# Small token group of a fused attention and expert kernel: the order of Vector and Scalar work within a slot

## The chip, the cores and the metric

The kernel runs on one core of one Trainium2 chip, in one launch. The metric is the device time of that core in microseconds (us). Five engines matter: TensorE (PE in the profile, with its weight loads PEld), VectorE (DVE), ScalarE (ACT), GpSimd (POOL, idle here) and SyncE (SP), which issues the DMAs. Each engine takes its instructions in the order in which the program gives them, and they meet through semaphores.

## What is computed

Attention through 32 packed tokens, then a dense layer with silu, then eight experts. A Sinkhorn iteration over all tokens gives the weight P of each token and expert.

```python
p_packed = sm_attn(p, k, v); out = sm_attn(q, p_packed, p_packed)     # 2304 x 512
h = x @ w_in;  x = (h * sigmoid(h)) @ w_out
P = exp(x @ w_gate - max)
for _ in range(8):
    P /= P.sum(1, keepdims=True) + 1e-9
    P /= P.sum(0, keepdims=True) + 1e-9
    P *= N / E
for e in range(8):
    out += P[:, e:e+1] * (max(x @ w1[e], 0) @ w2[e])
```

All of it is float32. The kernel gets the accuracy from pairs of float32r matmul operands: a tile is split into `hi` (a cast by ACT) and `lo` (raw minus `hi`, by DVE).

## The kernel before

The stages follow each other: attention with the start of the dense layer, the dense layer, the **small group** (from 374 to 560 us of the span), and then two groups of 1024 tokens with a Strassen-like scheme of seven products to the end. Only the small group is changed. In the dense layer a preparation `pre0` makes the first pieces for it.

The small group is 256 tokens (two tiles of 128). It runs 16 steps s = 0 to 15, one for each expert e = s // 2 and half fh = s % 2 of the hidden width. Each step has four slots, 0 to 3, and a piece number j = slot // 2. The order of all instructions of PE, DVE and ACT is the order of the Python code here (a manual schedule).

- PE, slots 0 and 2: `up0(s, j)`, 32 matmuls (L1011 with 512 columns, L1014 with 256) into a PSUM tile `u`. PE, slots 1 and 3: `down0(s-1, j)`, 12 matmuls (L1046) into `d`: the two hidden pieces `h` of the step before, in the order hi, hi, lo for each quarter of the width.
- `sum0(s, j)`, in slots 0 and 2: ACT copies half of `u` into `us` (L1020), DVE adds the other half (L1021).
- `relu0(s, j)`, in slots 1 and 3: ACT writes the relu of `us` as the hi part of `h` (L1030), DVE writes its lo part (L1031). The second piece, h(s, 1), is made in slot 3 of step s, and the first matmul that needs its lo part is the ninth of `down0(s, 0)` in slot 1 of step s + 1.
- Weight pieces: `w1_split` and `w2_split` give one piece a slot: an ACT cast (`w1h`, `w2h`, L144), a DVE subtraction (`w1l`, `w2l`, L145), and the DMA that loads the next raw piece. The piece made in slot 0 is w1(s+1, 1), in slots 1 and 2 w2(s, 0) and w2(s, 1), in slot 3 w1(s+2, 0).
- `sinkhorn` is a generator `sk` that moves on by one piece in every odd slot from step 1 on. In steps 2 to 6 a piece is: PE sums the columns of P with a matmul (`cs`, L1259), DVE takes the reciprocal `rc` (L1261, L1262), scales P (L1263), sums rows (L1252 to L1254), scales again (L1255) and sums columns (`csum`, L1256), which the next `cs` matmul reads half a step later. The row sum of iteration 0 has to wait for ACT's exp of P (L1248).
- `acc`: after `down0` with an odd s - 1, ACT copies `d` (experts 0 to 2, L1053) or DVE adds P times `d` (from expert 3 on, L1061; L1058 and L1060 collect the older ones in step 8).
- `x_forms`, a generator `xg`, from step 8 on in slots 1 to 3: DVE differences `xr` (L956 to L965), an ACT cast to `xf` (L977) and a DVE subtraction for its lo part (L978), for the next token group.

In the order before, an odd slot of a step holds: `down0` with its `acc`, the Sinkhorn piece, the weight piece, `relu0`, the piece of `xg`. An even slot holds `up0`, the weight piece, `sum0`, the piece of `xg`.

Of the kernel before, what the change touches and what calls it, by code (L numbers as in the profile page):

```python
# [9 lines left out]
F32 = mybir.dt.float32  # L10
# [4 lines left out]
ALU = mybir.AluOpType  # L15
# [89 lines left out]
def fused_kernel(  # L105
# [15 lines left out]
    pe, dve, act = nc.tensor, nc.vector, nc.scalar  # L121

    def pool(name, bufs, **kw):
        st = ExitStack()
        return st.enter_context(tc.tile_pool(name=name, bufs=bufs, **kw)), st
# [14 lines left out]
    def unit(shape, dt, name):  # L140
        return wp.tile(shape, dt, tag="w", name=name)

    def split(hi, lo, raw, eng=dve):
        act.copy(out=hi, in_=raw)  # L144
        eng.tensor_tensor(out=lo, in0=raw, in1=hi.bitcast(F32), op=ALU.subtract)  # L145
# [607 lines left out]
    G0 = 2 * NE  # L753
# [10 lines left out]
    raw1, raw2, wf, xf = {}, {}, {}, {}  # L764
# [8 lines left out]
    def load_w1(s, kh):  # L773
        _, e, fh = steps[s]
        t = st["r1"].tile([128, 2, FH], F32, tag="r1", name=f"r1_{s}{kh}")
        nc.sync.dma_start(t, w1[e, 256 * kh:256 * kh + 256, FH * fh:FH * fh + FH]
                          .rearrange("(c p) f -> p c f", p=128))
        raw1[s, kh] = t
# [64 lines left out]
    w1t, w2t = {}, {}  # L843

    def halves(name, s, j, raw):
        h = unit([128, 2, 512], F32R, f"{name}h{s}{j}")
        l = unit([128, 2, 512], F32R, f"{name}l{s}{j}")
        split(h, l, raw)
        return h, l

    def w1_split(s):
        w1t[s] = []
        for j in range(2):
            w1t[s].append(halves("w1", s, j, raw1[s, j]))
            if s + 1 < G0:
                load_w1(s + 1, j)
            yield
# [31 lines left out]
    def w2_split(s):  # L889
        w2t[s] = []  # L890
        for j in range(2):
            w2t[s].append(halves("w2", s, j, raw2[s, j]))
            if s + 1 < G0:
                load_w2(s + 1, j)
            yield
# [93 lines left out]
    xs, h0, done0 = [], {}, set()  # L989

    w1s = {s: w1_split(s) for s in range(G0)}
    w2s = {s: w2_split(s) for s in range(G0)}

    def pre0():

        xs.append(st["xx"].tile([128, 4, 2, 256], F32R, tag="xx", name="xs"))
        for k in range(4):
            for n, (sb, c, _) in enumerate(T0):
                o = slice(128 * n, 128 * n + 128)
                split(xs[0][:, k, 0, o], xs[0][:, k, 1, o], x2[sb][k][:, c:c + 128])  # L1000
            yield
        for g, n in ((w1s, 0), (w1s, 0), (w2s, 0), (w2s, 0), (w1s, 1)):
            next(g[n])
            yield

    def up0(s, j):
        ps = st["u0"].tile([128, 2, 512], F32, tag="u0", name=f"u0{s}{j}")
        for i in range(2):
            f = slice(128 * (2 * j + i), 128 * (2 * j + i) + 128)
            for k in range(4):  # L1010
                pe.matmul(ps[:, i], w1t[s][k // 2][0][:, k % 2, f], xs[0][:, k].rearrange("p l n -> p (l n)"),  # L1011
                          start=(k == 0), stop=(k == 3), skip_group_check=True)
            for k in range(4):
                pe.matmul(ps[:, i, 0:256], w1t[s][k // 2][1][:, k % 2, f], xs[0][:, k, 0],  # L1014
                          start=False, stop=(k == 3), skip_group_check=True)
        h0[s, j] = ps

    def sum0(s, j):
        u0, ps = st["S"].tile([128, 2, 256], F32, tag="S", name=f"us{s}{j}"), h0[s, j]
        act.copy(out=u0, in_=ps[:, :, 256:])  # L1020
        dve.tensor_tensor(u0, ps[:, :, 0:256], u0, op=ALU.add)  # L1021
        h0[s, j] = u0

    def relu0(s, j):
        if (s, j) in done0:
            return
        done0.add((s, j))
        u0 = h0[s, j]
        t = st["gh"].tile([128, 2, 2, 256], F32R, tag="gh", name=f"h0{s}{j}")
        act.activation(t[:, 0], u0, AF.Relu)  # L1030
        dve.scalar_tensor_tensor(t[:, 1], u0, 0.0, t[:, 0].bitcast(F32), op0=ALU.max, op1=ALU.subtract)  # L1031
        h0[s, j] = t
# [3 lines left out]
    def down0(s, tt):  # L1036
        _, e, fh = steps[s]
        if fh == 0:
            ps0[tt] = p3.tile([128, 512], F32, tag="y", name=f"d0{s}{tt}")
        ps = ps0[tt]  # L1040
        n = 0
        for f in range(4):
            wh, wl = w2t[s][f // 2]
            h = h0[s, f // 2]
            for l, w in ((0, wh), (0, wl), (1, wh)):
                pe.matmul(ps, h[:, l, f % 2, 128 * tt:128 * tt + 128], w[:, f % 2],  # L1046
                          start=(fh == 0 and n == 0), stop=(fh == 1 and n == 11))
                n += 1
        if fh == 0:
            return  # L1050
        if e < LATE:
            acc[e, tt] = st["acc"].tile([128, DM], F32, tag="acc", name=f"acc{e}{tt}")
            act.copy(out=acc[e, tt], in_=ps)  # L1053
            return
        pr = prob["P"][:, T0[tt][2], :]
        dst = acc[0, tt]
        if e == LATE:
            dve.tensor_scalar_mul(dst, dst, pr[:, 0:1])  # L1058
            for i in range(1, LATE):
                dve.scalar_tensor_tensor(dst, acc[i, tt], pr[:, i:i + 1], dst, op0=ALU.mult, op1=ALU.add)  # L1060
        dve.scalar_tensor_tensor(dst, ps, pr[:, e:e + 1], dst, op0=ALU.mult, op1=ALU.add)  # L1061
        if e == NE - 1:
            nc.sync.dma_start(out[128 * tt:128 * tt + 128, :], dst)
# [270 lines left out]
    with tc.manual_schedule(engines={mybir.EngineType.PE, mybir.EngineType.DVE, mybir.EngineType.Activation}):  # L1334
        for i, (c, b) in enumerate(seq):
# [14 lines left out]
            for half in range(2):  # L1350
# [25 lines left out]
                while len(tiles) > keep:  # L1376
                    n = tiles.pop(0)
# [46 lines left out]
    with tc.manual_schedule(engines={mybir.EngineType.PE, mybir.EngineType.DVE, mybir.EngineType.Activation}):  # L1424
        sk = sinkhorn()
        next(sk)
        for g in (1, 2):
            for k in range(4):
                tc.keep_in_program_order(nc.sync.dma_start(
                    x2d[k, :, TOK[g]:TOK[g] + 2 * NB],  # L1430
                    x2[2 - g][k][:, TOK[g] % SB:TOK[g] % SB + 2 * NB]))
        for s_ in (a2a_st, x2a_st, x2b_st, gt_st, hp_st, pt_st, pg_st):
            s_.close()
        for name, n in (("xf", 7), ("cp", 5), ("xr", 2), ("pb", 2)):
            open_(name, n, side="left", keep=True)
        open_("acc", 2 * LATE)
        st["u0"], u0_st = pool("pu", 2, space=PSUM, side="left", reuse_waits="tile")

        def chain(*gens):
            for g in gens:  # L1440
                yield from g

        xg = x_forms(1, x_keep, 3)
        for s in range(G0 + 1):
            for slot in range(4):
                if slot % 2 == 0:
                    if s < G0:
                        up0(s, slot // 2)
                elif s > 0:
                    if s == 2 * LATE + 2 and slot == 1:  # L1450
                        for _ in sk:
                            pass
                    down0(s - 1, slot // 2)
                if s == G0:
                    continue
                if s >= 1 and slot % 2:
                    next(sk, None)
                g, n = ((w1s, s + 1), (w2s, s), (w2s, s), (w1s, s + 2))[slot]
                if n < G0:
                    next(g[n], None)  # L1460
                if slot % 2 == 0:
                    sum0(s, slot // 2)
                if slot % 2 or s == G0 - 1:
                    relu0(s, slot // 2)
                if s >= 8 and slot:
                    next(xg, None)
            if s == G0 - 2:
                for _ in xg:
                    pass
            if s == G0 - 2:  # L1470
                for p in ORD[:2]:
                    w1_block(G0, p, "S")
            if s == G0 - 3:
                load_pb(1, 0)
            if s == G0 - 1:
                for p in ORD[:AHEAD]:
                    w1_get(G0, p)
        for name in ("acc", "r2", "gh", "xx", "po"):
            closers[name].close()
        u0_st.close()  # L1480
        st["m"], s_ = pool("pm", 2, space=PSUM, side="left", reuse_waits="tile"); ctx.enter_context(s_)
        for name, n in (("hb", 6), ("hi", 3), ("lo", 3), ("rb", 2)):
            open_(name, n, keep=True)
        forms = chain(*(w2_forms(s) for s in range(G0, 2 * G0)))
        xg2 = [x_forms(2, x_store)]
        moe_step(G0)
# [56 lines left out]
```

## Time and profile before

| | |
|---|---|
| time, median of 3 runs | 1785.2 us (1785.18 to 1785.34) |
| the profiled execution's own time | 1785.38 us |
| its span (first to last instruction) | 1783.6 us |
| PE busy | 1767.4 us, 99% of the span |
| PE weight loads | 1495.9 us, 84% |
| DVE busy | 1455.1 us, 82% |
| ACT busy | 1083.8 us, 61% |
| granted TensorE clock | 0.999 |

Matmuls are pipelined, and their ends are modelled: a matmul of 512 columns shows some 390 ns, while the next one starts 230 ns later. So PE can be late without showing idle time; the distance from one start to the next tells more. On DVE, too, an instruction that waits for nothing starts up to 0.09 us before the recorded end of the one before it.

### The profile page before, as it was taken

Reading aid. Unit: us, or ns where it says so; the run is one execution under the profiler, and the core shown is the slowest. Engines: PE = TensorE matmul, PEld = TensorE weight load, DVE = VectorE, ACT = ScalarE, POOL = GpSimd, SP = SyncE. Lnnn points to the kernel's source line nnn. Section 1 sums busy time; section 2 is a strip of 40 time slices with the busy share of each in tenths; the row PEclk is TensorE's granted clock in tenths of the full one; section 3 lists DMA queues with packets and bytes.
Section 4 is the critical chain, followed back from the end, with each engine's and each line's share of the span. In section 5 each row is a group of like instructions: output and inputs, shape, how many; then the busy total and the mean of one; then the engine's idle time right before and its main releaser. Section 6 shows DMA issues by size and latency. Waiting matters only on the chain.

```text
span 1783.6 us, 24891 instructions
## 1 busy us (share of the span) xinstructions
PE 1767.4 (99%) x9324; PEld 1495.9 (84%) x9324; DVE 1455.1 (82%) x1950; ACT 1083.8 (61%) x1726; POOL 1.0 (0%) x8
## 2 busy tenths in 40 slices
PE   8999999999999999999999999999999999999998
PEld 5899999987888888888888888888888888888887
DVE  7968796769886988999889999887777777777778
ACT  6766675655654666665666666656555555555555
POOL 0000000000000000000000000000000000000000
PEclk9999999999999999999999999999999999999999
DMA  9326676975764655465554455964455444545442
GB/s 359 132 95 214 248 264 248 334 251 167 227 199 166 226 182 187 160 197 190 195 168 171 172 182 197 323 224 166 155 176 158 161 154 147 168 157 170 149 130 94
DMA packets 141496, 341.72 MB, mean 192 GB/s; under 512 B 11952, under 2 KB 49472, under 8 KB 140480
## 3 DMA queue, kind: packets, MB, share of 16 engines
q1 hardware_dynamic: 141376, 340.14, 56.1%
q8 instruction: 73, 1.20, 0.3%
q14 instruction: 47, 0.39, 0.1%
HBM read 256.66 MB, written 83.44 MB: 191 GB/s over the span
## 4 chain that ended last, share of the span: by engine, by line
PE 91%; DVE 5%; ACT 1%; DMA 1%; issue 1%; SPq 0%; DVEq 0%; ACTq 0%
PE d L1134 34%; PE X L1182 20%; PE Z L1182 10%; PE g2w L689 8%; PE g L600 5%; PE Y L1182 5%; PE d L1046 3%; PE g L654 3%; PE u L1011 2%; PE u L1014 1%; DVE w2l L145 1%; PE u L193 1%; DMA kq<-in_kT_dram 1%; DVE w1l L145 0%; DMA rawin<-in_moe_w_in_dram 0%
## 5 line engine op out<-in xcount | busy, mean ns | idle before, releaser
L145 DVE TENSOR_TENSOR lo<-hb,hi 128x1024 fp32r<-128x1024 f32 x224 | 273.6, 1221 | 33.2 <-ACT hi L144 32.3
L1134 PE MATMUL d<-hi,w2f 128*128 128x512 f32 x896 | 294.2, 389 | 0.0
L1182 PE MATMUL X<-xf,w1l 128*128 128x512 f32 x1152 | 276.9, 389 | 0.0
L144 ACT CAST hi<-hb 128x1024 fp32r<-128x1024 f32 x224 | 235.3, 1052 | 65.3 <-PE d L1134 60.0
L1182 PEld LDWEIGHTS X<-xf,w1l 128*128 128x128 f32 x1152 | 216.2, 188 | 44.9
L1142 ACT COPY M<-d 128x512 f32<-128x512 f32 x234 | 137.3, 588 | 143.6 <-PE d L1134 140.6
L1146 DVE TENSOR_TENSOR M<-d,M 128x512 f32<-128x512 f32 x204 | 140.2, 688 | 101.3 <-PE d L1134 101.3
L1134 PEld LDWEIGHTS d<-hi,w2f 128*128 128x128 f32 x896 | 168.1, 188 | 34.8
L1134 PE MATMUL d<-lo,w2f 128*128 128x512 f32 x448 | 174.3, 389 | 0.0
L1134 PE MATMUL d<-hi,w2l 128*128 128x512 f32 x512 | 167.7, 389 | 0.0
L689 PE MATMUL g2w<-ring,woh 128*128 128x384 f32 x576 | 147.5, 337 | 0.0
L1130 ACT COPY d<-M 128x512 f32<-128x512 f32 x216 | 127.1, 589 | 20.4 <-DVE M L1146 19.0
L1134 PE MATMUL d<-hi,w2g 128*128 128x512 f32 x384 | 125.7, 389 | 0.0
L1134 PEld LDWEIGHTS d<-hi,w2l 128*128 128x128 f32 x512 | 96.1, 188 | 20.4 <-ACT d L1130 0.4
L689 PEld LDWEIGHTS g2w<-ring,woh 128*128 128x128 f32 x576 | 102.9, 188 | 8.6 <-issue 7.5
L1189 ACT COPY cp<-X 128x512 f32<-128x512 f32 x128 | 74.3, 581 | 47.1 <-PE X L1182 46.9
L1134 PE MATMUL d<-lo,w2l 128*128 128x512 f32 x256 | 99.6, 389 | 0.0
L1134 PEld LDWEIGHTS d<-lo,w2f 128*128 128x128 f32 x448 | 84.2, 188 | 17.4
L1182 PE MATMUL Y<-xf,w1f 128*128 128x512 f32 x384 | 97.3, 389 | 0.0
L689 PE MATMUL g2w<-ring,wol 128*128 128x384 f32 x288 | 96.3, 334 | 0.0
L144 ACT CAST w1f<-rb 128x512 fp32r<-128x512 f32 x96 | 59.8, 624 | 55.9 <-PE d L1134 41.3
L1182 PE MATMUL X<-xf,w1f 128*128 128x512 f32 x384 | 92.2, 389 | 0.0
(222 smaller groups left out, 3428.0 us busy)
## 6 DMA issues: line engine op xcount, KB each, us to landing
r<-in_moe_w_dram SPq DMA_DIRECT2D x128, 512.0 KB, 4.2
w1l<-w1d SPq DMA_DIRECT2D x128, 512.0 KB, 3.8
w1d<-po SPq DMA_DIRECT2D x64, 512.0 KB, 4.3
w2d<-w2f SPq DMA_DIRECT2D x64, 512.0 KB, 4.1
w2l<-w2d SPq DMA_DIRECT2D x64, 512.0 KB, 3.5
rb<-in_moe_w_dram SPq DMA_DIRECT2D x96, 256.0 KB, 2.6
sb<-in_moe_w_dram SPq DMA_DIRECT2D x48, 256.0 KB, 2.7
pb<-pd SPq DMA_DIRECT2D x16, 512.0 KB, 5.1
```

What stands on the lines that cost most here:

```text
L144: act.copy(out=hi, in_=raw)
L145: eng.tensor_tensor(out=lo, in0=raw, in1=hi.bitcast(F32), op=ALU.subtract)
L600: pe.matmul(ps, lhs[:, fs], rhs, start=(n == 0), stop=(n == 5))
L654: pe.matmul(ps[:, :HS], lhs, rhs, start=(n == 0), stop=(n == 3 * nf - 1))
L689: pe.matmul(ps[:, :TW], lhs[:, f % 2, ds], ring[f // 2][:, 2 * (f % 2) + rhs, q], start=(n == 0 and not on), stop=(n == 11), skip_group_ch ...
L1046: pe.matmul(ps, h[:, l, f % 2, 128 * tt:128 * tt + 128], w[:, f % 2], start=(fh == 0 and n == 0), stop=(fh == 1 and n == 11))
L1130: act.copy(out=ps, in_=m)
L1134: pe.matmul(ps, w[:, l, c, 128 * d:128 * d + 128], r[:, c], start=(n == 0 and not seed), stop=(n == 5), skip_group_check=seed)
L1142: act.copy(out=m, in_=ps)
L1146: dve.tensor_tensor(m, ps, m, op=ALU.add)
L1182: pe.matmul(ps, w[:, l, c, 128 * i:128 * i + 128], x[:, r, c], start=(n == 0 and p in (1, 7)), stop=(n == 5), skip_group_check=p in (2, 6, ...
L1189: act.copy(out=t, in_=ps)
```

## The change

The split of a weight piece becomes two generator steps: ACT's cast, then the DVE subtraction with the next load. A slot now holds, in program order: `up0` (even slots), the cast of the weight piece, `relu0` (odd slots), the subtraction of the weight piece, the piece of `xg`, `sum0` (even slots), and last, in odd slots, `down0` with its `acc` and the Sinkhorn piece. `pre0` calls each generator twice, so that its instructions stay as they were.

```diff
     def halves(name, s, j, raw):
-        split(h, l, raw)
+        act.copy(out=h, in_=raw)
+        yield
+        dve.tensor_tensor(out=l, in0=raw, in1=h.bitcast(F32), op=ALU.subtract)
         return h, l
...
-            w1t[s].append(halves("w1", s, j, raw1[s, j]))
+            w1t[s].append((yield from halves("w1", s, j, raw1[s, j])))
...
         for g, n in ((w1s, 0), (w1s, 0), (w2s, 0), (w2s, 0), (w1s, 1)):
+            next(g[n])
             next(g[n])
             yield
...
             for slot in range(4):
-                if slot % 2 == 0:
-                    if s < G0:
-                        up0(s, slot // 2)
-                elif s > 0:
+                odd, j = slot % 2, slot // 2
+                g, n = ((w1s, s + 1), (w2s, s), (w2s, s), (w1s, s + 2))[slot]
+                g = g[n] if n < G0 else iter(())
+                if s < G0:
+                    if not odd:
+                        up0(s, j)
+                    next(g, None)
+                    if odd:
+                        relu0(s, j)
+                    next(g, None)
+                    if s >= 8 and slot:
+                        next(xg, None)
+                    if not odd:
+                        sum0(s, j)
+                        if s == G0 - 1:
+                            relu0(s, j)
+                if odd and s > 0:
                     if s == 2 * LATE + 2 and slot == 1:
                         for _ in sk:
                             pass
-                    down0(s - 1, slot // 2)
-                if s == G0:
-                    continue
-                if s >= 1 and slot % 2:
-                    next(sk, None)
-                g, n = ((w1s, s + 1), (w2s, s), (w2s, s), (w1s, s + 2))[slot]
-                if n < G0:
-                    next(g[n], None)
-                if slot % 2 == 0:
-                    sum0(s, slot // 2)
-                if slot % 2 or s == G0 - 1:
-                    relu0(s, slot // 2)
-                if s >= 8 and slot:
-                    next(xg, None)
+                    down0(s - 1, j)
+                    if s < G0:
+                        next(sk, None)
```

The order of PE's own matmuls stays as it was; only numbers of buffers differ. What moves is DVE and ACT. DVE between two `csum` of the Sinkhorn steps (slot 3 of step 2 to slot 1 of step 3), before:

```order
L1256 TENSOR_REDUCE csum<-P 128x8
L145 TENSOR_TENSOR w1l_4769<-r_40_4651,w1h_4768 128x1024
L1031 SCALAR_TENSOR_TENSOR h_4774<-us_4740,h_4774 128x512
L145 TENSOR_TENSOR w1l_4795<-r_41_4677,w1h_4794 128x1024
L1021 TENSOR_TENSOR us_4800<-u_4777,us_4800 128x512
L1261 TENSOR_SCALAR rc<-cs_4816 128x8
```

The same place on DVE in the changed program:

```order
L1259 TENSOR_REDUCE csum<-P 128x8
L850 TENSOR_TENSOR w1l_4795<-r_41_4677,w1h_4794 128x1024
L1024 TENSOR_TENSOR us_4800<-u_4777,us_4800 128x512
L1034 SCALAR_TENSOR_TENSOR h_4806<-us_4800,h_4806 128x512
L850 TENSOR_TENSOR w2l_4804<-r_30_4689,w2h_4803 128x1024
L1264 TENSOR_SCALAR rc<-cs_4825 128x8
```

The kinds are the same five; `h` now stands directly behind the `us` that it is made from, where before the Sinkhorn piece and a weight piece stood between them.

ACT from the `us` copy of step 4, slot 0, before:

```order
L1020 COPY us_4918<-u_4895 128x512
L1053 COPY acc_4933<-d_4803 128x512
L144 CAST w2h_4946<-r_40_4831 128x1024
L1030 ACTIVATE h_4952<-us_4918 128x512
L144 CAST w2h_4972<-r_41_4857 128x1024
```

ACT there in the changed program:

```order
L1023 COPY us_4918<-u_4895 128x512
L848 CAST w2h_4921<-r_40_4810 128x1024
L1033 ACTIVATE h_4924<-us_4918 128x512
L1056 COPY acc_4942<-d_4812 128x512
L848 CAST w2h_4972<-r_41_4857 128x1024
```

ACT's copy of `d`, which needs the end of `down0`, has moved behind the cast and the relu.

DVE in step 10, from the `us` of its first piece to that of its second, before:

```order
L1021 TENSOR_TENSOR us_5574<-u_5551,us_5574 128x512
L1061 SCALAR_TENSOR_TENSOR acc_4694<-d_5473,P,acc_4694 128x512
L145 TENSOR_TENSOR w2l_5591<-r_100_5490,w2h_5590 128x1024
L1031 SCALAR_TENSOR_TENSOR h_5596<-us_5574,h_5596 128x512
L956 TENSOR_TENSOR xr_5392<-xr_5392 128x512
L978 TENSOR_TENSOR xf_5548<-xr_5393,xf_5548 128x512
L145 TENSOR_TENSOR w2l_5621<-r_101_5518,w2h_5620 128x1024
L1021 TENSOR_TENSOR us_5626<-u_5603,us_5626 128x512
```

And in the changed program, with the `h` behind the second piece:

```order
L1024 TENSOR_TENSOR us_5574<-u_5551,us_5574 128x512
L1034 SCALAR_TENSOR_TENSOR h_5580<-us_5574,h_5580 128x512
L850 TENSOR_TENSOR w2l_5578<-r_100_5480,w2h_5577 128x1024
L958 TENSOR_TENSOR xr_5376<-xr_5376 128x512
L980 TENSOR_TENSOR xf_5535<-xr_5377,xf_5535 128x512
L1064 SCALAR_TENSOR_TENSOR acc_4703<-d_5484,P,acc_4703 128x512
L850 TENSOR_TENSOR w2l_5621<-r_101_5518,w2h_5620 128x1024
L961 TENSOR_TENSOR xr_5376<-xr_5377,xr_5376 128x512
L980 TENSOR_TENSOR xf_5587<-xr_5376,xf_5587 128x512
L1024 TENSOR_TENSOR us_5630<-u_5603,us_5630 128x512
L1034 SCALAR_TENSOR_TENSOR h_5636<-us_5630,h_5636 128x512
```

`acc` has moved behind the x difference, the second difference and its `xf` have moved ahead of the second `us`, and again each `h` follows its `us`.

## Rows read from the trace of the kernel before

**Rows 1.** Page, engines: busy us (share of the span), instructions.
```profile
PE 1767.4 (99%) x9324; PEld 1495.9 (84%) x9324; DVE 1455.1 (82%) x1950; ACT 1083.8 (61%) x1726; POOL 1.0 (0%) x8
```

**Rows 2.** Waits of all engines, 365 to 560 us: total, times, longest.
```profile
PE d L1046 <- DVE h L1031: 2.5, 4, 1.0
```

**Rows 3.** Timeline of PE: start us, us, instruction, idle before it.
```profile
407.82 0.39 PE L1046 MATMUL d<-w2l,h 128*128 128x512 f32 x1
409.18 0.73 PE L1046 MATMUL d<-w2h,h 128*128 128x512 f32 x2 [0.97 <-DVE h L1031]
...
446.33 0.48 PE L1011 MATMUL u<-xs,w1h 128*128 128x512 f32 x1
...
463.29 0.61 PE L1011 MATMUL u<-xs,w1h 128*128 128x512 f32 x2
...
474.38 0.62 PE L1011 MATMUL u<-xs,w1h 128*128 128x512 f32 x2
...
514.10 0.74 PE L1046 MATMUL d<-w2h,h 128*128 128x512 f32 x2 [0.83 <-DVE h L1031]
...
548.74 0.62 PE L1011 MATMUL u<-xs,w1h 128*128 128x512 f32 x2
```

**Rows 4.** Chain that ended last, 400 to 450 us: start us, us, what.
```profile
401.30 1.22 DVE w2l L145
...
443.29 1.22 DVE w1l L145
...
445.16 1.20 PE d L1046 x4
```

**Rows 5.** Stretches: us, busy of PE, PEld, DVE, ACT, POOL; clock, DMA, GB/s.
```profile
404.70:446.70 42.00, 40.57 (x207) 33.30 (x206) 40.31 (x85) 22.25 (x31) 0.00 (x0) 1.00 0.57 178
466.90:547.00 80.10, 78.75 (x396) 65.91 (x395) 68.94 (x89) 47.94 (x69) 0.00 (x0) 1.00 0.63 193
```

**Rows 6.** Timeline of DVE, one round of the Sinkhorn steps.
```profile
410.77 0.16 DVE L1261 TENSOR_SCALAR rc<-cs 128x8 f32<-128x8 f32 x1
...
413.29 1.22 DVE L145 TENSOR_TENSOR w2l<-r,w2h 128x1024 fp32r<-128x1024 f32 x1
414.42 0.69 DVE L1031 SCALAR_TENSOR_TENSOR h<-us,h 128x512 fp32r<-128x512 f32 x1
415.02 1.22 DVE L145 TENSOR_TENSOR w2l<-r,w2h 128x1024 fp32r<-128x1024 f32 x1
416.16 0.69 DVE L1021 TENSOR_TENSOR us<-u,us 128x512 f32<-128x512 f32 x1
416.76 0.16 DVE L1261 TENSOR_SCALAR rc<-cs 128x8 f32<-128x8 f32 x1
```

**Rows 7.** Timeline of DVE in steps 2, 8, 14 and 15.
```profile
399.65 0.42 DVE L1252 TENSOR_REDUCE rsum<-P 128x18 f32<-128x144 f32 x1 [1.88 <-ACT P L1248]
...
466.94 0.69 DVE L1021 TENSOR_TENSOR us<-u,us 128x512 f32<-128x512 f32 x1 [1.64 <-ACT us L1020]
...
546.95 0.69 DVE L1031 SCALAR_TENSOR_TENSOR h<-us,h 128x512 fp32r<-128x512 f32 x1
...
548.17 0.68 DVE L1021 TENSOR_TENSOR us<-u,us 128x512 f32<-128x512 f32 x1
549.55 0.69 DVE L1031 SCALAR_TENSOR_TENSOR h<-us,h 128x512 fp32r<-128x512 f32 x1 [0.70 <-ACT h L1030]
```

**Rows 8.** Timeline of ACT in step 15.
```profile
548.88 0.63 ACT L1030 ACTIVATE h<-us 128x512 fp32r<-128x512 f32 x1 [1.49 <-DVE us L1021]
```

**Rows 9.** Waits of DVE, 466.9 to 547 us: total, times, longest.
```profile
DVE w1l L145 <- ACT w1h L144: 3.7, 5, 1.0
DVE w2l L145 <- ACT w2h L144: 3.5, 4, 1.0
DVE us L1021 <- ACT us L1020: 2.8, 3, 1.6
DVE acc L1061 <- PE d L1046: 2.4, 2, 1.4
```

More of the change, by code (lines that the diff above doesn't have):

```diff
@@ L891, in w2_split @@
         for j in range(2):
-            w2t[s].append(halves("w2", s, j, raw2[s, j]))
+            w2t[s].append((yield from halves("w2", s, j, raw2[s, j])))
             if s + 1 < G0:
```

## The prediction

> **What bounds the kernel now.** I read the page first. PE is busy 99% of the span [rows 1], so only two things can change the time: a wait that PE has in the small group, or one that it gets. The waits of all engines from 365 to 560 us come next. PE waits there four times, 2.5 us in all, each time for DVE's lo part of `h` [rows 2]. The timeline of PE shows what such a wait costs: between the starts at 407.82 and 409.18 lie 1.36 us, where the next matmul normally starts after 0.23, so 1.13 us are lost and 0.97 recorded [rows 3]. An undisturbed step takes 474.38 - 463.29 = 11.09 us [rows 3].
>
> The chain of waits says more than PE's idle time. From 401.30 to PE's restart at 445.16 it runs over DVE [rows 4]. In the stretch 404.7 to 446.7 DVE is busy 40.31 of 42.00 us [rows 5], and its timeline there shows a round of half a step that waits for nothing: from `rc` to `rc` 416.76 - 410.77 = 5.99 us [rows 6]. PE's restarts at 409.18 and 445.16 [rows 3, 4] lie 35.98 us apart, which is six such rounds (35.94). So in steps 3 to 6 **DVE sets the pace**, and PE's small waits are only where this shows. In steps 8 to 15 DVE is busy 68.94 of 80.10 us [rows 5] and has waits of its own [rows 9]; PE waits there too, as at 514.10 [rows 3].
>
> **The change part by part.** PE's own order stays; its matmuls cost the same.
>
> *What it removes.* The lo part of h(s, 1) no longer stands behind a Sinkhorn piece and a weight piece. From `us` to `h` the round of before takes 0.60 (us) + 2.52 (the piece, 410.77 to 413.29) + 1.13 (weight) = 4.25 us [rows 6]. The four waits of PE [rows 2] go as long as DVE is no later than now. If every delay of PE went: in steps 8 to 15 PE takes 548.74 - 463.29 = 85.45 us [rows 3] for seven and a half steps of 11.09, 83.18, so 2.3 is to be had there; in the Sinkhorn steps 1.1 for the first wait plus at most 3 x (11.98 - 11.09) = 2.7, part of which is PE's own `cs` matmuls. That makes 3.4 to 6.1; I take the middle, 4.7.
>
> *What it adds.* `h` on DVE needs ACT's relu, which needs DVE's `us`. Before, DVE worked on something else while ACT did that relu. Now `h` is the next DVE instruction, and DVE has nothing to do until it comes. The trace has this order at one place, step 15: `us` starts at 548.17, the relu at 548.88 (0.63 us), `h` at 549.55, with 0.70 us of recorded idle time [rows 7, 8]. Start to start that is 1.38 us, where a DVE that waits for nothing needs 0.60 (414.42 to 415.02, the same size of work) [rows 6]. **Each `h` therefore costs DVE 0.78 us more**, twice a step. Queued behind it on DVE are the weight piece, the Sinkhorn piece or the x pieces, and for these PE waits through `csum` and through the next `h`. Where DVE has slack this costs nothing; the rows above say that in steps 2 to 6 it has none.
>
> *Term A, the Sinkhorn steps.* The exp chain is left as it is: the row sum at 399.65 still waits for ACT's exp [rows 7], and the `csum` of iteration 0 ends as before, when DVE goes on at 401.30 [rows 4]. From there to the `csum` of iteration 7 before were seven rounds, 443.29 - 401.30 = 41.99 us [rows 4]. A round now is 5.99 + 0.78 = 6.77 us; seven are 47.4, so this `csum` ends at 448.7. PE's next `cs` matmul needs it, and behind `cs` stands `up0(6, 1)`, which began at 446.33 [rows 3]. PE reached `cs` on its own by then, so it waits: with 0.2 us for `cs` itself the start is 448.9, and **A = +2.6 us**. It is less than 7 x 0.78 = 5.5 because PE now meets DVE at `csum`, at the end of a round, and `h` comes early in it. Bounds: if the 0.78 were hidden, PE would be free and A would be -2.4 (the Sinkhorn half of the 4.7); if PE and DVE met no later than before, +5.5.
>
> *Term B, steps 8 to 15.* At `us` of step 8 (466.94) DVE had waited 1.64 us for PE's result [rows 7], so there it is again at PE's pace and B starts from zero. The end point is `h` of (14, 1) at 546.95 [rows 7], for which PE's `down0` waits before `up0(15, 1)` at 548.74 [rows 3]. These 80.0 us of DVE hold 12.4 - 1.64 = 10.8 us of recorded waits, 13 of them [rows 9]; each also loses the 0.09 by which an instruction otherwise starts before the recorded end of the last one (414.42 against 413.29 + 1.22 [rows 6]), so 12.0. In the new order:
> - 14 `h` at 0.78 each: +10.9.
> - At (10, 1), (13, 1) and (14, 1) an x difference now stands ahead of ACT's `us` copy, so DVE's `us` waits for `xf` and the copy. The like wait where a cast stands in the copy's place is 1.0 [rows 9], and the copy handles half the elements; so about 0.6 each, an estimate: +1.8.
> - One `acc` (the one of step 14, slot 3) moves behind the end point: -0.7.
> - Of the 12.0 old waits, those for PE's results and most of those for casts go, since DVE is later and ACT does its cast during the wait for the relu. Those stay where an x difference still stands ahead of a cast: I count five, two at 1.1 and three at 0.4 with `acc` between, 3.4 us. So -8.6.
>
> The sum is **B = +3.4 us**. With nothing saved but the recorded waits for PE it could be near +9; if DVE never came late, PE would lose its old waits and B = -2.3. I take +3.4: DVE's 69 us of work in 80 [rows 5] with 14 forced waits of 0.78 leave no slack.
>
> **Edits at nothing.** ACT's copy of `d` moves behind cast and relu; in the Sinkhorn steps DVE lags half a step behind ACT, which hides it, and without that cover DVE would wait for the late cast, up to 1.0 us a time, as it now does elsewhere [rows 9]. Loads of raw pieces are issued 0.6 us later in odd slots; the pieces are needed a step, 11 us, later. The `yield` in `pre0` moves no instruction.
>
> **Sum.** 1785.38 (the profiled execution's own time) + 2.6 + 3.4 = 1791.4 us; it stands 0.2 above the median of the runs, so 1791.2. Nothing behind step 15 gives it back, as PE is the bound there.
>
> A rule that would have it otherwise stands in the Trainium skill, Perfetto Trace Analysis, Optimization Strategy: find the gaps of the engine that one optimizes, see what blocks them, and make these dependencies start sooner. Read on PE, the engine with the highest occupancy here, it speaks for this change and gives the -4.7 of the first rival. The rows disagree as to which engine that is: the chain is DVE's in steps 3 to 6, and the page itself allows that the most contended engine changes over time. Against the change speaks what TensorE: Matmul & The Clock Gate, Architectural detail, says: the queues of ACT and DVE are strictly first in, first out; the 0.70 us of idle DVE with other work in line [rows 7] agrees.
>
> **The rivals.**
> 1. *The waits for `h` go and nothing comes in their place:* 1785.2 - 4.7 = 1780.5. For it: all four waits are for `h` [rows 2], and `h` is ready 4.25 - 1.38 = 2.9 us earlier after its `us`. Against it: DVE without slack. It decides where the 0.78 a half step is covered, that is if PE's half step with `cs` were over 6.77 us.
> 2. *Only the Sinkhorn steps lose:* in steps 8 to 15 the earlier `h` and the extra waits cancel, B between -2.3 and +1. Time 1785.5 to 1788.8, middle 1787.2. For it: DVE is idle 11 us of 80 there [rows 5, 9]. Against it: those waits are forced by ACT and partly remain.
> 3. *More is lost:* old waits stay in full, or ACT's copy of `d` holds up casts; B about +9, time 1797.
> 4. *Nothing to measure because the order does not bind:* excluded by rounds without a wait [rows 6], but for small cancellation, held in 2.
>
> **How the numbers follow.** Forecast (1788.8 to 1794.5, around 1791.2) 0.6; rival 2 0.2; rival 1 0.12; rival 3 0.08. A measurement of this kernel tells some 0.2%, 3.6 us, from no change. Slower by more: the forecast, rival 3 and a little of 2, less the forecast's lower edge, 0.66; within: 0.22; faster: 0.12. The range 1786.0 to 1794.5 leaves out rival 1, rival 3 and the edge of 2.
>
> **What would show it.** In the changed kernel's trace: DVE idle about 0.70 us before each `h`, ended by ACT (right: the added wait). PE's waits at `cs` for `csum`, about 1 us per half step from step 3 to 6, and none for `h` there; rounds of 6.77 us; `up0(6, 1)` at 448.9 (term A). In steps 8 to 15 PE waits for `h` in steps 12 and 15, 2 to 3 us each (term B); `up0(15, 1)` at about 554.7. The prediction is wrong if rounds stay near 6 us, or if PE never waits at `cs`.

## The result and the profile after

The changed kernel takes 1794.4 us (median of 6 runs, 1793.36 to 1795.64); the kernel before, run beside it, 1785.36 us. The ratio is 1.0051, 95% interval 1.0038 to 1.0064: **slower by 9.0 us**. The forecast was slower, +6.0 us.

The engines of the page after, in busy us (share of the span) and instructions, beside [rows 1]:

```profile
PE 1769.2 (99%) x9324; PEld 1495.9 (83%) x9324; DVE 1456.0 (81%) x1950; ACT 1083.5 (60%) x1726; POOL 1.0 (0%) x8
```

The instruction counts are those of before, so no engine has more work. The waits of all engines from 365 to 560 us (total, times, longest) say where the time is, and stand against the single group of PE before [rows 2]:

```profile
DVE h L1034 <- ACT h L1033: 22.7, 31, 1.3
...
PE d L1049 <- ACT h L1033: 5.7, 3, 2.7
...
PE cs L1262 <- DVE csum L1259: 3.5, 5, 0.7
```

DVE now waits 22.7 us in 31 places for the relu, and PE's waits have grown from 2.5 to 9.2 us. DVE's timeline (start us, us, instruction, idle before it) has one round of the Sinkhorn steps, to be laid beside [rows 6]:

```profile
412.45 0.16 DVE L1264 TENSOR_SCALAR rc<-cs 128x8 f32<-128x8 f32 x1
...
414.98 1.21 DVE L850 TENSOR_TENSOR w2l<-r,w2h 128x1024 fp32r<-128x1024 f32 x1
416.12 0.68 DVE L1024 TENSOR_TENSOR us<-u,us 128x512 f32<-128x512 f32 x1
417.49 0.69 DVE L1034 SCALAR_TENSOR_TENSOR h<-us,h 128x512 fp32r<-128x512 f32 x1 [0.70 <-ACT h L1033]
418.10 1.22 DVE L850 TENSOR_TENSOR w1l<-r,w1h 128x1024 fp32r<-128x1024 f32 x1
419.24 0.16 DVE L1264 TENSOR_SCALAR rc<-cs 128x8 f32<-128x8 f32 x1
```

From `rc` to `rc` it is 419.24 - 412.45 = 6.79 us where it was 5.99. Only `h` waits, for 0.70 us; from `us` to `h` it is 1.37 us, where work without a wait follows after 0.60.

PE's timeline where it waits:

```profile
421.87 0.39 PE L1262 MATMUL cs<-csum,ones 128*128 128x8 f32 x2 [0.69 <-DVE csum L1259]
...
449.17 0.71 PE L1014 MATMUL u<-xs,w1h 128*128 128x512 f32 x2
...
504.58 0.50 PE L1049 MATMUL d<-w2h,h 128*128 128x512 f32 x1 [0.83 <-ACT h L1033]
...
518.36 0.50 PE L1049 MATMUL d<-w2h,h 128*128 128x512 f32 x1 [2.15 <-ACT h L1033]
...
554.92 0.62 PE L1049 MATMUL d<-w2h,h 128*128 128x512 f32 x1 [2.72 <-ACT h L1033]
555.33 0.63 PE L1049 MATMUL d<-w2l,h 128*128 128x512 f32 x1
...
557.51 1.58 PE L1014 MATMUL u<-xs,w1h 128*128 128x512 f32 x4
```

`up0(6, 1)` starts at 449.17 instead of 446.33, `up0(15, 1)` at 557.51 instead of 548.74 [rows 3]. (All of the small group lies 0.13 us later in this execution, since its first `up0` starts at 374.23 and not 374.10; the differences below are less that.) The last three waits name ACT's relu as their end, not DVE's `h` as before: the lo part now follows the relu at once, so PE stops a few matmuls earlier, at the first one that reads the hi part.

Behind the wait of 2.72 us something else shows. The stretches of 1 us from 554 (us, busy of PE, PEld, DVE, ACT, POOL; granted clock, DMA, GB/s):

```profile
554.00:555.00 1.00, 0.08 (x1) 0.09 (x1) 0.30 (x2) 0.77 (x2) 0.00 (x0) 1.00 1.04 372
555.00:556.00 1.00, 1.00 (x3) 0.58 (x4) 1.00 (x2) 0.34 (x1) 0.00 (x0) 0.57 1.02 356
556.00:557.00 1.00, 1.00 (x3) 0.80 (x3) 1.00 (x3) 0.00 (x0) 0.00 (x0) 0.50 0.19 65
557.00:558.00 1.00, 1.00 (x4) 0.71 (x3) 0.45 (x1) 0.52 (x1) 0.00 (x0) 0.50 0.67 90
558.00:559.00 1.00, 1.00 (x5) 0.81 (x4) 0.69 (x1) 1.00 (x3) 0.00 (x0) 0.72 0.90 360
```

PE is busy all the time from 555 on, but at half the clock (1.2 instead of 2.4 GHz): its matmuls follow each other after 0.41 us (554.92, 555.33) where 0.23 is normal. The lost shares of these rows add up to 0.43 + 0.50 + 0.50 + 0.28 = 1.7 us of TensorE's work.

DVE's waits in steps 8 to 15, from 469.75 to 555 us, beside [rows 9]:

```profile
DVE h L1034 <- ACT h L1033: 10.6, 14, 1.3
DVE us L1024 <- ACT us L1023: 2.8, 4, 1.1
DVE w2l L850 <- ACT w2h L848: 1.8, 3, 1.0
DVE w1l L850 <- ACT w1h L848: 1.4, 2, 1.0
DVE acc L1064 <- DVE acc L1063: 0.5, 1, 0.5
```

### The profile page after: what moved, and what is told of

Read it like the earlier page. It is cut to its first block, busy times and chain, and to the rows that moved or that the text cites. A ratio compares the mean times of both kernels' runs of the same rounds, so it can differ in the third digit from the quotient of the medians.

```text
span 1792.8 us, 24865 instructions
## 1 busy us (share of the span) xinstructions
PE 1769.2 (99%) x9324; PEld 1495.9 (83%) x9324; DVE 1456.0 (81%) x1950; ACT 1083.5 (60%) x1726; POOL 1.0 (0%) x8
## 4 chain that ended last, share of the span: by engine, by line
PE 87%; DVE 9%; ACT 2%; issue 1%; DMA 1%; DVEq 0%; SPq 0%; ACTq 0%
PE d L1137 33%; PE X L1185 19%; PE Z L1185 10%; PE g2w L689 8%; PE g L600 5%; PE Y L1185 5%; PE g L654 3%; DVE w2l L850 2%; DVE w1l L850 1%; PE d L1049 1%; ACT h L1033 1%; DVE us L1024 1%; PE u L193 1%; PE u L1014 1%; DVE h L1034 0%
```

## The experiments

The theory: `h` directly behind its `us` costs DVE 0.78 us, because ACT's relu lies between them, and DVE has no slack. Rivals: that the rest of the order does it (the late Sinkhorn piece, ACT's copy of `d`, the x differences ahead of `us`), or that the clock does. The kernel before ran beside all of them, with medians of 1785.58 to 1785.73 us.

**1. Something between relu and `h`.** The changed kernel, with the weight subtraction put between ACT's relu and DVE's `h` in odd slots. All else stays; in step 15, the last, `relu0` runs through at once as in the changed kernel.

```diff
         act.activation(t[:, 0], u0, AF.Relu)
+        yield
         dve.scalar_tensor_tensor(t[:, 1], u0, 0.0, ...)
...
                     next(g, None)
-                    if odd:
-                        relu0(s, j)
+                    r = relu0(s, j) if odd else iter(())
+                    next(r, None)
                     next(g, None)
+                    next(r, None)
...
                         if s == G0 - 1:
-                            relu0(s, j)
+                            for _ in relu0(s, j):
+                                pass
```

> The changed order, but in an odd slot DVE does the weight piece between us and h (ACT's relu still comes before it). Forced-wait theory (DVE has nothing to do during ACT's relu): the 0.70 us gaps before h go in the Sinkhorn steps, a round falls from 6.77 back to 6.0 us, PE's waits at cs for csum shrink to under 0.2 us each, up0(6,1) starts near 444 instead of 449.2, and the time is 1780.5 to 1783, under both kernels. Rival (the Sinkhorn piece as the last of a slot makes csum late for PE): that place is unchanged here, so PE still waits about 0.7 us at each cs and the time stays over 1788.

Measured: 1781.27 us, 0.9975 of the kernel before (0.9965 to 0.9985). The stretches of the Sinkhorn steps and of steps 8 to 15:

```profile
405.60:447.00 41.40, 41.40 (x217) 35.36 (x217) 39.72 (x84) 22.69 (x31) 0.00 (x0) 1.00 0.54 175
470.00:548.00 78.00, 78.00 (x396) 66.09 (x395) 68.89 (x89) 48.53 (x68) 0.00 (x0) 1.00 0.65 212
```

PE is busy for the whole of both stretches (41.40 of 41.40 us, 78.00 of 78.00). DVE's timeline:

```profile
409.51 0.68 DVE L1024 TENSOR_TENSOR us<-u,us 128x512 f32<-128x512 f32 x1
410.11 1.22 DVE L850 TENSOR_TENSOR w2l<-r,w2h 128x1024 fp32r<-128x1024 f32 x1
411.24 0.68 DVE L1035 SCALAR_TENSOR_TENSOR h<-us,h 128x512 fp32r<-128x512 f32 x1
411.85 0.16 DVE L1265 TENSOR_SCALAR rc<-cs 128x8 f32<-128x8 f32 x1
```

`h` waits for nothing and stands 1.73 us behind its `us` instead of 1.37, and that 0.36 us later `h` makes the whole kernel 13.1 us faster than the changed one. The position of one instruction of 0.68 us decides the sign of the change. This version beats both kernels.

**2. The wait made longer.** The changed kernel with ACT's relu issued twice (the second writes the same values again).

```diff
         act.activation(t[:, 0], u0, AF.Relu)
+        act.activation(t[:, 0], u0, AF.Relu)
```

> The changed order with each relu on ACT issued twice (the output is the same). Forced-wait theory: each gap before h grows by one relu issue, 0.53 us; rounds of 7.30 us, up0(6,1) at about 452.9 instead of 449.2, the 14 pieces of steps 8 to 14 add up to 7.4 more; time 1803 to 1807. Rival (order of the Sinkhorn and x pieces alone, ACT being busy only 60%): within 1 us of 1794.4.

Measured: 1810.56 us, 1.0138 (1.0124 to 1.0152), 16.2 above the changed kernel and over the expected range. DVE's and ACT's timelines:

```profile
418.28 0.68 DVE L1024 TENSOR_TENSOR us<-u,us 128x512 f32<-128x512 f32 x1
420.32 0.69 DVE L1035 SCALAR_TENSOR_TENSOR h<-us,h 128x512 fp32r<-128x512 f32 x1 [1.36 <-ACT h L1034]
```

```profile
418.99 0.63 ACT L1033 ACTIVATE h<-us 128x512 fp32r<-128x512 f32 x1 [3.75 <-DVE us L1024]
419.66 0.63 ACT L1034 ACTIVATE h<-us 128x512 fp32r<-128x512 f32 x1
420.19 1.03 ACT L848 CAST w1h<-r 128x1024 fp32r<-128x1024 f32 x1
```

A second relu delays `h` by 0.67 us, not by the 0.53 after which the cast follows: it writes the same tile, and starts 0.04 us behind the recorded end of the first. From `us` of step 8 (476.23) to `h` of (14, 1) (569.68) DVE takes 93.45 us, 8.3 more than in the changed kernel; `up0(6, 1)` comes at 454.61, 5.7 later once the two executions' starts (374.00, 374.23) are set equal. Another 1.0 us lies between these two places, so `h` of (14, 1) comes 15.0 us later. The two profiled executions differ by 14.9 us (1809.5 and 1794.61), the medians by 16.2. In this trace TensorE's clock is at half in three places, behind waits of 3.08, 1.91 and 4.71 us. So the time follows the wait, in the Sinkhorn steps and after them.

**3 and 4. The change in one half of the steps alone.** The new order up to step 7 and that of before from step 8 on (what stands in the added branch), and the other way round, with `s < 8` in the condition.

```diff
+                if s >= 8:
...
+                    continue
                 if s < G0:
```

> The changed order in steps 0 to 7, the order of before from step 8 on. If the two terms add up, only the Sinkhorn term is left: up0(6,1) at 449.2, steps 8 to 15 shifted as they were, no low granted clock near 555; time 1785.4 + 2.7 = 1788.1. Rival (all of the loss comes from the x pieces): 1785.4.

> The order of before in steps 0 to 7, the changed order from step 8 on. If the two terms add up: us of step 8 where it was, h of (14,1) about 5.1 us later than before, PE idle some 2.7 us before it and then a stretch at half the granted clock that costs 1.7; time 1785.4 + 6.3 = 1791.7, and 1790 if the clock stays up. Rival (all of the loss comes from the Sinkhorn steps): 1785.4.

Measured: 1788.37 us (1.0014, 1.0005 to 1.0023) and 1789.96 us (1.0024, 1.0015 to 1.0033). Against the 1785.73 of the kernel before that is +2.6 and +4.2. In the first, PE's `up0(6, 1)` stands at

```profile
449.68 0.71 PE L1014 MATMUL u<-xs,w1h 128*128 128x512 f32 x2
```

which is 2.71 us late (with a first `up0` at 374.74), as in the changed kernel. In the second, DVE takes 84.27 us from `us` of step 8 to `h` of (14, 1), 4.3 more than before. The parts make 6.9 us of the 9.0 that both cost together. Where the rest lies was not tested. Three places of the changed kernel's trace that kernel 4 does not have would cover it, with some 2.7 us for the 2.1 that are missing: DVE's first `h` of step 8 waits 1.29 us and not 0.78, since the cast ahead of its relu waited for a DMA (kernel 8, with the same order there, does not have this wait); an `acc` waits 0.46 us for the one before it; and the clock falls at the last wait, not in step 12.

**5. Only the Sinkhorn piece moved.** The kernel before, its Sinkhorn piece last in the odd slot.

```diff
-                if s >= 1 and slot % 2:
-                    next(sk, None)
...
                 if s >= 8 and slot:
                     next(xg, None)
+                if s >= 1 and slot % 2:
+                    next(sk, None)
```

> The kernel before with one part of the change: the Sinkhorn piece moves to the end of the odd slot; relu and weight pieces stay where they were. Forced-wait theory: no gap arises (a weight piece stands between us and h), rounds stay 5.99 us, h comes 2.5 us earlier and PE's four waits in steps 3 to 6 go; steps 8 to 15 stay as before; time 1785.7 - 2.4 = 1783.3. Rival (a Sinkhorn piece at the end makes PE wait for csum): PE waits at cs, time 1788 or more.

Measured: 1784.96 us, 0.9996 (0.9987 to 1.0005): no gain that can be told, where 1783.3 was expected. The timelines of ACT and DVE in step 2:

```profile
397.56 0.59 ACT L1053 COPY acc<-d 128x512 f32<-128x512 f32 x1 [2.18 <-PE d L1046]
398.04 1.05 ACT L144 CAST w2h<-r 128x1024 fp32r<-128x1024 f32 x1
```

```profile
399.12 1.22 DVE L145 TENSOR_TENSOR w2l<-r,w2h 128x1024 fp32r<-128x1024 f32 x1 [3.02 <-ACT w2h L144]
...
402.91 0.30 DVE L1256 TENSOR_REDUCE csum<-P 128x8 f32<-128x144 f32 x1
```

ACT's copy of `d` waits 2.18 us for the end of `down0`, the cast stands behind it and DVE's subtraction behind the cast. The Sinkhorn piece is now queued behind all this, and DVE goes on behind the first `csum` at 403.13 instead of 401.30 [rows 4], 1.6 us late if the two starts of the stage (374.35, 374.10) are set equal. The rounds then run on at about 6 us, with no wait for the relu. So what kept this order from its gain should be the copy of `d` ahead of the cast.

**6. Only the relu's parts moved.** The kernel before, `relu0` ahead of the Sinkhorn and the weight piece in odd slots.

```diff
+                if slot % 2:
+                    relu0(s, slot // 2)
                 if s >= 1 and slot % 2:
                     next(sk, None)
...
-                if slot % 2 or s == G0 - 1:
+                if s == G0 - 1:
                     relu0(s, slot // 2)
```

> The kernel before with the other part: relu0 goes ahead of the Sinkhorn piece and the weight piece in odd slots, nothing else moves. Forced-wait theory: DVE waits 0.70 us for each relu, the rounds become 6.77 us, up0(6,1) starts near 449 as in the changed kernel; with the gaps of steps 8 to 15 the time is 1790 to 1795. Rival (only the Sinkhorn piece's place or the x pieces cost): within 1 us of 1785.7, or faster, because h is earlier.

Measured: 1792.08 us, 1.0034 (1.0022 to 1.0047). Here the Sinkhorn piece and ACT's copy of `d` stay ahead of the weight piece, the weight piece isn't split and no x difference moves ahead of a sum; still 6.5 us are lost. DVE's timeline:

```profile
411.98 0.69 DVE L1031 SCALAR_TENSOR_TENSOR h<-us,h 128x512 fp32r<-128x512 f32 x1 [0.70 <-ACT h L1030]
412.59 0.16 DVE L1261 TENSOR_SCALAR rc<-cs 128x8 f32<-128x8 f32 x1
...
419.36 0.16 DVE L1261 TENSOR_SCALAR rc<-cs 128x8 f32<-128x8 f32 x1
```

The same 0.70 us, and the same round of 6.77.

**7. The x piece behind the sum.** The changed kernel with the piece of `xg` behind `sum0` in even slots, so that no x difference stands ahead of ACT's `us` copy.

```diff
                     next(g, None)
+                    if not odd:
+                        sum0(s, j)
                     if s >= 8 and slot:
                         next(xg, None)
                     if not odd:
-                        sum0(s, j)
                         if s == G0 - 1:
```

> The changed order with the piece of x_forms behind sum0 again in even slots. The us of (10,1), (13,1) and (14,1) no longer waits for ACT's xf, 0.57 us each; but in ACT's queue xf and the next cast then stand ahead of the relu, so h of the same piece waits longer. Worked out from the changed kernel's rows: from the end of w2l to h 3.45 us instead of 3.33, so no gain: within 1 us of 1794.4. Rival (the x piece ahead of the sum is what costs in steps 8 to 15): 1790 or less, and no low granted clock.

Measured: 1793.12 us, 1.004 (1.0027 to 1.0052), 1.3 below the changed kernel, with intervals that overlap. DVE's waits from 469 to 556 us:

```profile
DVE h L1034 <- ACT h L1033: 10.3, 12, 1.6
DVE w2l L850 <- ACT w2h L848: 1.8, 3, 1.0
DVE w1l L850 <- ACT w1h L848: 1.4, 2, 1.0
DVE us L1024 <- ACT us L1023: 1.1, 1, 1.1
```

The waits of `us` behind an x difference are gone (the one left is the first `us` of step 8), but `h` now waits up to 1.6 us behind them: ACT gets to the relu later. The wait changes its place, and little is gained, if anything.

**8. One x piece less ahead of the last wait.** The changed kernel without the piece of `xg` in slot 2 of step 14; it is done at the end of that step.

```diff
-                    if s >= 8 and slot:
+                    if s >= 8 and slot and (s, slot) != (G0 - 2, 2):
```

> The changed kernel, with one x piece (step 14, slot 2) left to the end of that step. On DVE h(14,1) then comes 1.25 us earlier (no x difference, xf or wait for the us copy ahead of us), so PE's wait before the end of the small group falls from 2.7 to about 1.5 us. If the stretch at half the granted clock follows from that long wait and costs 1.7 us, it goes too: time 1794.4 - 1.25 - 1.7 = 1791.5. If the clock costs nothing here: 1793.1.

Measured: 1792.56 us, 1.004 (1.0027 to 1.0053), between the two. DVE's `h` of (14, 1) is there at 553.40, PE does not wait for it, and `up0(15, 1)` follows 1.79 us later, at full clock. But the half clock has moved to step 12. PE's timeline there, and the stretches:

```profile
518.72 0.54 PE L1049 MATMUL d<-w2h,h 128*128 128x512 f32 x1 [2.12 <-ACT h L1033]
519.06 0.63 PE L1049 MATMUL d<-w2l,h 128*128 128x512 f32 x1
```

```profile
518.00:519.00 1.00, 0.28 (x1) 0.28 (x2) 0.30 (x2) 0.96 (x2) 0.00 (x0) 1.00 0.75 272
519.00:520.00 1.00, 1.00 (x3) 0.51 (x3) 1.00 (x2) 1.00 (x3) 0.00 (x0) 0.52 1.02 389
520.00:521.00 1.00, 1.00 (x4) 0.77 (x3) 1.00 (x2) 1.00 (x2) 0.00 (x0) 0.50 0.87 348
```

In step 12 the fall costs this kernel nothing that shows. One fall is 1.7 us of lost work, 0.001 of the span; the execution with a mean granted clock of 1.000, which cannot have had one, took 1792.85 us, and two with 0.998 took 1792.56.

The median alone does not tell whether the fall at the last wait of the changed kernel costs 1.7 us, but the traces do so for the two profiled executions. Counted from the first `up0` (375.07, 374.23), DVE's `h` of (14, 1) is 2.3 us sooner than in the changed kernel (0.5 of it because the wait behind the DMA in step 8 is not there) and PE's `up0(15, 1)` at 555.19 is 3.2 us sooner. The 0.8 beyond `h` is what PE lost at half clock up to there, 1.2 us, less 0.4 that it restarted earlier. Behind `up0(15, 1)` the moved piece takes 0.8 us back: from there to the next stage PE needs 11.8 us and not the 11.0 of the kernel before, where it has to wait for `h` of step 15. At the stage's end 2.9 us are left. The median is only 1.8 us lower; in the profiled execution the small group began 0.8 us later than in the changed kernel's, before anything that the edit touches.

**9. Kernel 1's order in the Sinkhorn steps alone**, that of before from step 8 on (an edit like that of kernel 3, on kernel 1).

> The order of the filled kernel (weight piece between us and h, down0 with ACT's copy of d behind the cast and the relu, the Sinkhorn piece last) in steps 0 to 7, the order of before from step 8 on. If what kept the Sinkhorn piece alone from its 2.4 us was ACT's copy of d ahead of the cast (first csum 1.6 us later), it is gone here: first csum 27.0 us after the first u, PE without waits in steps 3 to 6, time 1785.6 - 2.4 = 1783.2. If the Sinkhorn steps have no more to give: 1785.

Measured: 1783.23 us, 0.9988 (0.9979 to 0.9997). The Sinkhorn piece is last in the slot as in kernel 5, but ACT's copy of `d` stands behind cast and relu. ACT's timeline and DVE's first `csum`, beside those of kernel 5:

```profile
396.05 1.05 ACT L848 CAST w2h<-r 128x1024 fp32r<-128x1024 f32 x1
397.00 0.63 ACT L1033 ACTIVATE h<-us 128x512 fp32r<-128x512 f32 x1
398.34 0.59 ACT L1057 COPY acc<-d 128x512 f32<-128x512 f32 x1 [0.70 <-PE d L1050]
```

```profile
402.11 0.30 DVE L1260 TENSOR_REDUCE csum<-P 128x8 f32<-128x144 f32 x1
```

The first `csum` starts 402.11 - 375.13 = 26.98 us after the first `up0`, in kernel 5 402.91 - 374.35 = 28.56 us. So the place of the copy is what kernel 5 lacked. Kernel 1 gains 4.5 us against the kernel before, this kernel 2.4, so by difference some 2 us of kernel 1's gain belong to the steps behind the Sinkhorn steps.

## Why the prediction was right in its direction and too low

**DVE sets the pace, and each `h` costs it 0.78 us: right.** It shows in the rounds of 6.79 us, in kernel 6, which moves little else, and in kernel 1, where the loss goes when the round trip through ACT is covered. A longer wait (kernel 2) costs more.

**Term A: right.** `up0(6, 1)` came 2.71 us late (2.6 predicted), and kernel 3, with nothing but this half, lost 2.6 us. PE waits at `cs` for `csum` as forecast, though the waits recorded are 0.7 us each where "about 1 us per half step" stood; it does not wait for `h` there any more.

**Term B: right in kind, too small.** +3.4 was predicted and DVE took 554.90 - 469.78 = 85.1 us where it took 80.0, so +5.1. By the same items, each wait with 0.09 added: the 14 `h` cost 11.9 and not 10.9, mostly for the one in step 8 behind the DMA; the `us` waits 2.0 (from the second on) and not 1.8; the casts keep 3.6 and not 3.4; and 0.55 is a wait of one `acc` for the one before it, which was not foreseen. Together these are 1.9 above the forecast, 0.2 more than there is to explain. The loads issued later, put down at nothing, may have cost the 0.6 of that one `h`; in kernels 4 and 8 it waits 0.78.

**The step that failed** is that the way from this `h` to `up0(15, 1)` and to the stage's end would stay as it was. The last matmul of `down0` ends at 569.17 us and not 559.90, 9.1 us late, while DVE's `h` is 7.8 late. Two things lie between: 1.7 us of PE's work at half clock, and about 0.4 back, because PE restarts with the relu and not with the lo part. 2.7 + 5.1 + 1.7 - 0.4 = 9.1, where 9.0 was measured. The 1.7 is read from one execution, and kernel 8's trace bears it out; that it belongs to the median too was not shown apart. The measured 1794.4 lies 0.1 us under the upper edge of the stated range. The mechanism carries most of the 9.0; that the clock's 1.7, which the prediction does not have, did not take the number over this edge was luck.

**"Waits for `h` in steps 12 and 15 of 2 to 3 us each": right** (2.15 and 2.72), with one of 0.83 in step 11 besides. **ACT's copy of `d` moved "at nothing": too simple.** By kernels 5 and 9 its new place is worth 1.6 us at the first `csum`, once the Sinkhorn piece is last; the two edits only pay together.

The first rival, 1780.5, priced what is to be had if the 0.78 is covered. Kernel 1 covers it and takes 1781.27. The rule of the Trainium skill, Perfetto Trace Analysis, Optimization Strategy, to make the dependency behind a gap start sooner, leads astray when it is read on PE alone: of the kernel before, kernel 1 and the changed kernel, the last makes `h` follow its `us` soonest (4.25 us in [rows 6], 1.73 and 1.37), and it is the slowest.

## What to carry to other kernels

On an engine that has no slack, do not put an instruction directly behind the one whose result must first go through another engine; put work that is ready between them, at least as long as the wait would be (here 1.22 us of work for 0.70 us of idle time). In kernel 1 a consumer that comes 0.36 us later costs nothing, as PE still has work, while in the changed kernel an idle 0.7 us twice a step delays all that is queued behind it. When one reorders such a queue, the pieces are to be moved together and read by the row that ends each wait: the Sinkhorn piece last gained nothing before ACT's copy had moved too.

## What the hardware showed that was not expected

TensorE's granted clock falls to half, 1.2 GHz, in or behind single waits of an engine that is 99% busy; in the changed kernel's rows from 555 to 559 us such a stretch costs 1.7 us of its work. In the changed kernel it fell after 2.72 us of idle time, and after 2.15 us in the same execution it did not; after 2.12 us in kernel 8 it did, and after 1.56 us in kernel 7, too. The waits of 0.7 us in the Sinkhorn steps did not lower it (granted clock 1.00 from 405.6 to 447 us of the changed kernel). When it falls was not settled here. The Trainium skill, TensorE: Matmul & The Clock Gate, Part 1, says that a block that watches how busy the engine has been sets the clock, and calls the number of matmuls that run slow at a kernel's start "run-variable"; the rows agree with the first, as each fall inside the kernel stands in or behind a wait, and what they show in mid-kernel is as variable: in step 12 it stayed up in one kernel and fell in another. The price depends on what comes next: in kernel 4 it fell in a wait of 2.12 us in step 12, and PE still had to wait 1.53 us for `h` in step 15, so the lost work would have been a longer wait there. In the changed kernel PE waits no more behind the fall, and the loss stays.

Two relus in a row on the same tile start 0.67 us apart, where another instruction follows 0.53 us behind a relu.
